# Attention beside a gated MLP: dense products on the whole TensorE array instead of four column tiles, and the second norm's scale spread by TensorE

## The chip, the cores and the metric

The kernel runs on one core of a Trainium2 chip. The time is device time in microseconds from the start to the end of the program on that core. Before the change it is 1151.72 us, the median of two runs (1150.81 and 1152.64). The core's engines run side by side, each with its own instruction stream in a fixed order: TensorE (PE, matrix products; its weight loads are listed apart as PEld), VectorE (DVE), ScalarE (ACT), GpSimd (POOL) and SyncE (SP), which here issues all DMAs. They wait for each other through semaphores.

## The reference, cut to what matters

There are 2048 tokens of 1024 features, in bf16. The input is normed once, and the result goes through an attention with 32 heads of 32 features and, normed a second time, through an MLP with 3584 hidden features. The MLP's output gates that of the attention.

```python
xn = layernorm(x)                                   # 2048 x 1024
q, k, v = split(xn @ wqkv)                          # 32 heads, 32 features each
p = softmax(q @ k.T * 32 ** -0.5)                   # per head, 2048 x 2048
s = (p @ v, heads side by side) @ wo
y = layernorm(xn)
h = gelu(y @ w1 + b1)                               # 2048 x 3584
g = silu(h @ w2 + b2)
out = x + s * g
```

The mean of xn is zero and its variance is known from the first norm, so the second norm is one factor per token. The kernel computes it from the first norm's statistics.

## The kernel before, in words

**Layout.** Activations are kept transposed, features on the partitions and tokens along the row: `xnT` (in the buffer `big`), `yT` (the second norm of 256 tokens), `hT` (hidden features). The 32 heads are handled in 8 groups of 4, since four heads of 32 features fill 128 partitions.

**Dense products.** All products with weight matrices (Q, K and V projections, `w1`, `w2`, `wo`) go through the helper `quad` (line 578). It cuts the 128 output partitions of one product into four column tiles of 32 and issues four matmuls at `tile_position=(0, 32 * j)`, each with 128 contracted rows, 32 weight columns and the same 256 or 512 moving columns. Each matmul has a weight load of its own. `quad` is also used where four heads really differ: for P times V (line 930) and for the column sums of P (`ones`, lines 939 and 942). The trace shows all of these as L580, told apart by the names of their tiles. The scores (line 912) run in row tiles, 32 rows by 128 columns for each of the four heads. The transposes of the start (line 691) use the whole array.

**Attention.** `unit` (line 901) is one step: four heads, 256 queries, 256 keys. It has eight score matmuls, two exponentials of 1024 elements per partition on ScalarE (line 921), one addition on VectorE that halves the work of the column sums (line 924), eight PV matmuls and four sum matmuls. There are 512 units. For each head group and block of 256 queries (64 in all) the PV and sum matmuls of eight units follow as one burst into one bank of PSUM; then `norm` (line 949) divides.

**MLP.** For each chunk of 256 tokens `make_y` (line 763) multiplies `xnT` by the second norm's factor into `yT`, `w1_item` (line 771) makes 256 hidden features at a time, with bias and GELU on VectorE and ScalarE, and `w2_item` (line 802) sums over all hidden features into 256 outputs, with the gate. The weights are read again for each chunk, through rings of three (`w1r`) and four (`w2r`) buffers.

**The second norm's factor and the biases.** GpSimd computes the factor for all tokens at the end of the start (lines 728 to 732), one token per partition and one column per block of 128 tokens. `yT` needs it along the row, the same on all partitions. So line 733 stores it to DRAM, token after token (`s_scratch`), and `make_y` reads 256 of them back, spread over all partitions, into the one buffer `sbc` (line 764). Line 734 reads the bias `b1` element by element into a layout with features on partitions (`b1T`), and line 735 reads `b2` to all partitions. These DMAs are issued on SyncE's queue in the order of the plan.

**What sets the order.** The program is not written in the order of its execution. Every instruction is registered with an estimate of its duration, its reads and its writes, and `_Plan.run` (line 78) places all of them by a list schedule on the host, each engine's stream in the order in which its instructions were placed. On TensorE a score step comes before a PV or sum step, and that before a dense step (a "chunk", mostly two quads). Score steps are held back while the dense work is behind its even share of all units. Each step on TensorE has a mode, "c" for column tiles, "r" for row tiles, "t" for the transposes; where it differs from the last one's, the planner adds 100 ns (line 278). Dense work and PV bursts both have the mode "c". From the end of the start on, PV bursts and dense items share two banks of PSUM, six are kept for scores. The semaphore waits follow from the order (`settle`, line 336), so the order is fixed before the kernel runs, whatever the durations on the chip.

## Time and profile before

| | |
|---|---|
| median of the runs | 1151.72 us (1150.81 to 1152.64) |
| the profiled execution's own time | 1151.67 us |
| its span, first to last instruction of the program | 1140.5 us |
| mean granted TensorE clock over the span | 0.991 |
| TensorE | 29,984 matmuls and as many weight loads |
| VectorE, ScalarE | 1543 and 1186 instructions |
| DMA | 159.55 MB, 140 GB/s over the span |

How to read the lines shown below. A group's line gives the source line, engine, operation, the tiles written and read with their shapes (partitions x elements, for matmuls rows*columns of the tile of the array used), how many there are, the busy time in us, the mean duration of one in ns, and the idle time of the engine just before them with what ended it. A line of the timeline gives start and length in us, engine, line, operation and count, and in brackets the idle time before it and its cause. A line of the waits gives who waited for whom, the total in us, how often, and the longest. A line of the windows gives a stretch, its length, each engine's busy time with its instructions (TensorE, weight loads, VectorE, ScalarE, GpSimd), the mean granted TensorE clock, and DMA. "issue" is time in which an engine waited for nothing that the profile shows. The line numbers are those of the kernel before. Matmuls overlap, so a matmul's duration is longer than the distance to the next.

### The profile page before, as it was taken

To read this page: it belongs to the slowest core of one execution; us is meant where nothing else is said; L and a number is where in the kernel's file an instruction comes from. 1 tells how busy PE (TensorE), PEld (TensorE's weight loads), DVE (VectorE), ACT (ScalarE), POOL (GpSimd) and SP (SyncE) were. 2 spreads that over 40 slices of the span, in tenths; PEclk is the share of its full clock that TensorE was granted. 3 is DMA by queue.
4 is the path that set the end of the run, shared out by engine and by line. 5 is a ranking of instruction groups with operands and counts; after the bars stand their busy time and mean duration, and the time that the engine had idled before them with its cause. 6 is when DMAs were issued, how large, how long until landed. Compare 5 with 4: busy or idle time off the path is not lost.

```text
span 1140.5 us, 63544 instructions
## 1 busy us (share of the span) xinstructions
PE 1046.8 (92%) x29984; PEld 714.6 (63%) x29984; DVE 853.4 (75%) x1543; ACT 1039.5 (91%) x1186; POOL 32.7 (3%) x42
## 2 busy tenths in 40 slices
PE   5769999999989999999999899999999998789997
PEld 4545666667766667667666567657766666566443
DVE  6559877687778867886669776976679777756786
ACT  3759989999989999999999999999999999879993
POOL 5600000000000000000000000000000000000000
PEclk9979999999999999999999999999999999899999
DMA  8243376434564556443555546533365458464442
GB/s 250 67 107 109 94 199 169 115 95 117 145 169 135 144 142 191 120 113 95 148 163 141 142 136 172 160 92 109 83 179 158 121 154 256 150 189 122 132 131 85
DMA packets 289268, 159.55 MB, mean 140 GB/s; under 512 B 28912, under 2 KB 278768, under 8 KB 289008
## 3 DMA queue, kind: packets, MB, share of 16 engines
q1 hardware_dynamic: 289008, 155.49, 47.8%
q8 instruction: 235, 3.85, 1.5%
q14 instruction: 25, 0.20, 0.1%
HBM read 143.40 MB, written 12.07 MB: 136 GB/s over the span
## 4 chain that ended last, share of the span: by engine, by line
PE 63%; ACT 27%; DVE 4%; issue 3%; SPq 1%; POOL 1%; DMA 1%; POOLq 0%; ACTq 0%
PE ps L580 53%; ACT P L921 25%; PE ps L912 10%; ACT ut L795 2%; DVE stats L704 1%; SPq L735 1%; DVE xb L787 1%; DVE nt L951 1%; POOL gw L718 0%; ACT gw L828 0%; DMA sbc<-s_scratch 0%; DVE V L653 0%; POOLq L1057 0%; DMA hT<-in_A_x_dram 0%; SPq L734 0%
## 5 line engine op out<-in xcount | busy, mean ns | idle before, releaser
L921 ACT ACTIVATE P<-ps 128x1024 bf16<-128x1024 f32 x1024 | 970.4, 1087 | 69.4 <-PE ps L912 47.0
L924 DVE TENSOR_TENSOR PA<-P 128x1024 bf16<-128x1024 bf16 x512 | 348.6, 688 | 117.5 <-ACT P L921 92.9
L580 PE MATMUL ps<-yT,w1r 128*32 128x256 bf16 x7168 | 235.9, 274 | 10.2 <-issue 6.7
L580 PE MATMUL ps<-w2r,hT 128*32 128x256 bf16 x7168 | 230.3, 273 | 8.6 <-issue 5.4
L580 PEld LDWEIGHTS ps<-yT,w1r 128*32 128x32 bf16 x7168 | 179.5, 97 | 52.9 <-issue 35.5
L580 PEld LDWEIGHTS ps<-w2r,hT 128*32 128x32 bf16 x7168 | 181.2, 97 | 41.7 <-issue 32.4
L580 PE MATMUL ps<-P,V 128*32 128x256 bf16 x4096 | 161.6, 276 | 12.1 <-DVE V L653 8.6
L580 PE MATMUL ps<-big,qk 128*32 128x512 bf16 (+1 forms) x2208 | 133.7, 369 | 5.4 <-DVE xb L787 3.1
L580 PE MATMUL ps<-qk,big 128*32 128x256 bf16 (+1 forms) x2944 | 126.4, 307 | 6.2 <-ACT big L694 2.0
L580 PEld LDWEIGHTS ps<-P,V 128*32 128x32 bf16 x4096 | 109.5, 98 | 28.0 <-DVE V L653 9.3
L912 PE MATMUL ps<-qk 32*128 32x256 bf16 x2048 | 105.0, 275 | 21.8 <-ACT P L921 14.8
L580 PE MATMUL ps<-PA,ones 128*32 128x256 bf16 x2048 | 120.7, 275 | 3.2 <-issue 3.0
L912 PE MATMUL ps<-QKT 32*128 32x256 bf16 x2048 | 102.7, 273 | 11.5 <-ACT P L921 9.8
L580 PEld LDWEIGHTS ps<-qk,big 128*32 128x32 bf16 x2944 | 72.6, 97 | 40.9 <-issue 14.3
L787 DVE TENSOR_TENSOR xb<-ps,b1T 128x512 bf16<-128x512 f32 x112 | 76.8, 686 | 18.7 <-PE ps L580 17.7
L580 PEld LDWEIGHTS ps<-big,qk 128*32 128x32 bf16 x2208 | 53.8, 97 | 53.4 <-issue 13.7
L912 PEld LDWEIGHTS ps<-qk 32*128 32x128 bf16 x2048 | 31.3, 92 | 87.8 <-ACT P L921 58.6
L797 DVE SCALAR_TENSOR_TENSOR hT<-ut,xb 128x512 bf16<-128x512 f32 x112 | 76.4, 684 | 9.5 <-ACT ut L795 9.3
L912 PEld LDWEIGHTS ps<-QKT 32*128 32x128 bf16 x2048 | 30.7, 92 | 81.1 <-ACT P L921 67.2
L795 ACT ACTIVATE ut<-ut 128x512 f32<-128x512 f32 x112 | 77.8, 698 | 2.8 <-DVE ut L793 2.8
L793 DVE SCALAR_TENSOR_TENSOR ut<-sq,xb 128x512 f32<-128x512 bf16 x112 | 76.7, 686 | 1.7
L580 PEld LDWEIGHTS ps<-PA,ones 128*32 128x32 bf16 x2048 | 55.6, 97 | 19.3 <-issue 16.9
(50 smaller groups left out, 443.8 us busy)
## 6 DMA issues: line engine op xcount, KB each, us to landing
w1r<-in_B_w_dram SPq DMA_DIRECT2D x112, 512.0 KB, 4.3
w2r<-in_B_w_dram SPq DMA_DIRECT2D x128, 448.0 KB, 4.5
qk<-in_A_wqkv_dram SPq DMA_DIRECT2D x16, 256.0 KB, 3.6
g_scratch<-gw SPq DMA_DIRECT2D x32, 128.0 KB, 2.7
o_scratch<-ot SPq DMA_DIRECT2D x56, 64.0 KB, 3.1
big<-o_scratch SPq DMA_DIRECT2D x7, 512.0 KB, 7.3
hT<-in_A_x_dram SPq DMA_DIRECT2D x10, 256.0 KB, 5.4
qk<-in_A_wqkv_dram SPq DMA_DIRECT2D x4, 512.0 KB, 4.5
```

Of the source, the lines that this page charges most:

```text
L580: ins = e.matmul(dst(j), lhsT=lhsT(j), rhs=rhs(j), start=start, stop=stop, tile_position=(0, 32 * j), skip_group_check=True)
L704: dve(lambda e, t=t, c=c: e.bn_stats(stats[:, t, c, :], xst[t][:, c * 512:(c + 1) * 512]), 600, [XS(t)], [("st", t, c)], 1)
L735: dma("b2", lambda e: e.dma_start(b2b[:], B_b2.rearrange("(o d) -> o d", o=1).to_broadcast([128, D])), 262144, [("s3",)], [("b2",)])
L787: dve(lambda e: e.tensor_tensor(xb_t[i3][:].rearrange("p (k t) -> p k t", k=2), bank(it.bank).rearrange("p (k t) -> p k t", k=2), b1T[:, 2 ...
L793: dve(lambda e: e.scalar_tensor_tensor(ut_t[i3][:], sq_t[p % 2][:], 1.0 / GA, xb_t[i3][:], op0=ALU.add, op1=ALU.mult), c_f32(512), [("sq", ...
L795: act(lambda e: e.activation(ut_t[i3][:], ut_t[i3][:], ACT.Tanh, scale=GC * GA), c_act(512), [("ut", i3)], [("ut", i3)], 1)
L797: dve(lambda e: e.scalar_tensor_tensor(hT[:, hs].rearrange("p k t -> p (k t)"), ut_t[i3][:], 1.0, xb_t[i3][:], op0=ALU.add, op1=ALU.mult), ...
L912: ins = e.matmul(bank(b0[j], kk * 256, (kk + 1) * 256), lhsT=QKT[sl][32 * j:32 * j + 32, 1, kb * 128:(kb + 1) * 128], rhs=QKT[sl][32 * j:3 ...
L921: x = act(lambda e, h=h: e.activation(P[pi][:, 2 * h:2 * h + 2].rearrange("p j k q -> p (j k q)"), ps[:, pr[h] * 1024:(pr[h] + 1) * 1024], ...
L924: pa = dve(lambda e: e.tensor_tensor(PA[ai][:], P[pi][:, :, 0, :], P[pi][:, :, 1, :], op=ALU.add), c_b16(1024), [("P", pi, 0), ("P", pi, 1 ...
L951: a = dve(lambda e: e.transpose(nt_t[i][:], bank(pv.bank, 256, 512)), c_ps(256), [], [("nt", i)], 1, pv)
```

## The change

1. Every dense product (V, Q and K projections, `w1`, `w2`, `wo`) is one matmul on the whole array, 128 weight columns, through a new helper `full`, in place of four on column tiles. PV and the sums keep `quad`. The dense chunks' mode becomes "f", that of the transposes too. PV and sums keep "c".
2. The second norm's factor no longer goes through DRAM. For each block of 128 tokens VectorE multiplies an f32 identity by the factor (a diagonal, `dg`), TensorE multiplies it by a matrix of ones in f32 (two matmuls of 128 columns into one bank), and VectorE copies the result to `sbc`. This is an item of the MLP's queue, once for each of the eight chunks.
3. `b1` is read as 28 rows of 128 into `b1r`, which needs only the identity to be ready in the plan, is transposed on TensorE, and copied to `b1T`.

```diff
-        s_d = nc.dram_tensor("s_scratch", (S,), F32).ap()
...
+        b1r = sb("b1r", [FB, 128], BF16)
+        identf = sb("identf", [128, 128], F32)
+        onesf = sb("onesf", [128, 128], F32)
+        dg = sb("dg", [128, 2, 128], F32)
...
-        def chunk(item, fn, occ, R, mode="c", W=()):
+        def chunk(item, fn, occ, R, mode="f", W=()):
...
+        def full(e, dst, lhsT, rhs, start, stop):
+            return e.matmul(dst, lhsT=lhsT, rhs=rhs, start=start, stop=stop, skip_group_check=True)
...
+        dve(lambda e: e.tensor_single_scalar(identf[:], iota_i[:], 0, op=ALU.is_equal), 220, [("iota",)], [("identf",)], 2)
+        dve(lambda e: e.memset(onesf[:], 1.0), 140, [], [("onesf",)], 2)
...
-                        ins = quad(e, lambda j: bankp(b, j, t2 * 256, (t2 + 1) * 256),
-                                   lambda j: xnT[:, dc, tb * 128 + 32 * j:tb * 128 + 32 * j + 32],
-                                   lambda j: wv[:, dc, :], dc == 0, dc == DC - 1)
+                        ins = full(e, bank(b, t2 * 256, (t2 + 1) * 256), xnT[:, dc, tb * 128:(tb + 1) * 128],
+                                   wv[:, dc, :], dc == 0, dc == DC - 1)
...
-            chunk(it, fn, 620, [("xnb", t % 4), ("ident",)], mode="t")
+            chunk(it, fn, 620, [("xnb", t % 4), ("ident",)])
...
-        dma("s_st", lambda e: e.dma_start(s_d.rearrange("(t p) -> p t", p=128), lnp[:, :, 3]), 8192, [("s3",)], [("s_d",)])
-        dma("b1", lambda e: e.dma_start(b1T[:], B_b1.rearrange("(fb p) -> p fb", p=128)), 8192, [("s3",)], [("b1",)])
+        dma("b1", lambda e: e.dma_start(b1r[:], B_b1.rearrange("(fb p) -> fb p", p=128)), 8192, [("ident",)], [("b1r",)])
...
+        def b1_item():
+            it = _Item("mlp")
+            chunk(it, lambda e, b: e.transpose(bankb(b)[:, 0:FB], b1r[:], ident[0:FB, 0:FB]), 60, [("b1r",), ("ident",)])
+            dve(lambda e: e.tensor_copy(b1T[:], bankb(it.bank)[:, 0:FB]), c_ps(FB), [], [("b1",)], 0, it)
+            mq.append(it)
+
         def make_y(c):
-            dma("sbc", lambda e: e.dma_start(sbc[:], s_d[c * 256:(c + 1) * 256].rearrange("(o d) -> o d", o=1).to_broadcast([128, 256])),
-                131072, [("s_d",)], [("sbc",)])
+            for i in range(2):
+                dve(lambda e, i=i: e.tensor_scalar_mul(dg[:, i, :], identf[:], lnp[:, 2 * c + i, 3:4]), 140,
+                    [("s3",), ("identf",)], [("dg", i)], 2)
+            it = _Item("mlp")
+
+            def fn(e, b):
+                for i in range(2):
+                    ins = full(e, bank(b, i * 128, (i + 1) * 128), onesf[:], dg[:, i, :], True, True)
+                return ins
+            chunk(it, fn, 500, [("dg", 0), ("dg", 1), ("onesf",)])
+            dve(lambda e: e.tensor_copy(sbc[:], bank(it.bank, 0, 256)), c_ps(256), [], [("sbc",)], 0, it)
+            mq.append(it)
...
         for s_ in seq_mlp():
             if s_[0] == "y":
+                if s_[1] == 0:
+                    b1_item()
                 make_y(s_[1])
```

The other dense products (the pairs of Q and K in the start, `w1`, `w2`, `qk_item`, `wo`) change from `quad` to `full` as the V product above does.

More of the change, by code (lines that the diff above doesn't have):

```diff
@@ L781, in fn @@
                     for dc in dcs:
[L782 to L784 removed]
+                        ins = full(e, bank(b, f2 * 256, (f2 + 1) * 256), w1r[gi][:, dc, f2 * 128:(f2 + 1) * 128],
+                                   yT[:, dc, :], dc == 0, dc == DC - 1)
                     return ins
```

22 lines of the change are left out of this document (7 added, 15 removed).

## The prediction

> **What bounds the kernel now.** I read the page first (span, busy shares, the chain that ended last), then the waits by engine, then the timeline around the longest waits.
>
> ```profile
> span 1140.5 us, 63544 instructions
> PE 1046.8 (92%) x29984; PEld 714.6 (63%) x29984; DVE 853.4 (75%) x1543; ACT 1039.5 (91%) x1186; POOL 32.7 (3%) x42
> q8 instruction: 235, 3.85, 1.5%
> PE 63%; ACT 27%; DVE 4%; issue 3%; SPq 1%; POOL 1%; DMA 1%; POOLq 0%; ACTq 0%
> ```
>
> TensorE and ScalarE are both over 90% busy, and the chain runs mostly over TensorE. So a microsecond of TensorE counts, until ScalarE has no gap left. How much ScalarE gives is in the waits. The first two rows are its waits from 140 to 1040 us, the others TensorE's and one of VectorE's in the whole span:
>
> ```profile
> ACT P L921 <- PE ps L912: 32.7, 46, 4.7
> ACT P L921 <- PE ps L580: 7.5, 12, 1.9
> ...
> PE ps L912 <- ACT P L921: 24.6, 34, 1.9
> PE ps L580 <- issue: 17.3, 29, 1.4
> ...
> PE ps L912 <- issue: 7.3, 9, 3.3
> DVE yT L767 <- DMA sbc<-s_scratch: 13.5, 1, 13.5
> ```
>
> In the long middle ScalarE waits 32.7 + 7.5 = 40.2 us for TensorE. That is the most that a lighter TensorE can win there. TensorE itself loses 17.3 + 7.3 = 24.6 us to "issue", where no semaphore held it. One of those stops is the 3.3 us in the start, the other 21.3 us lie in the middle and end.
>
> What those stops are is seen where two follow each other (timeline of TensorE):
>
> ```profile
> 956.46 0.28 PE L580 MATMUL ps<-PA,ones 128*32 128x256 bf16 x1 [1.26 <-issue]
> 956.47 0.50 PE L580 MATMUL ps<-P,V 128*32 128x256 bf16 x8
> 956.69 0.71 PE L580 MATMUL ps<-PA,ones 128*32 128x256 bf16 x16
> 957.33 0.40 PE L912 MATMUL ps<-qk 32*128 32x256 bf16 x8
> 957.66 1.71 PE L580 MATMUL ps<-w2r,hT 128*32 128x256 bf16 x56
> 959.30 0.40 PE L912 MATMUL ps<-qk 32*128 32x256 bf16 x8
> 959.63 0.51 PE L580 MATMUL ps<-w2r,hT 128*32 128x256 bf16 x12
> 959.97 0.71 PE L580 MATMUL ps<-yT,w1r 128*32 128x256 bf16 x18
> 962.07 0.61 PE L580 MATMUL ps<-yT,w1r 128*32 128x256 bf16 x14 [1.39 <-issue]
> ```
>
> Both stops fall inside a group of four (18 is not a multiple of 4), where the program has no wait. Between them lie 1 + 8 + 16 + 8 + 56 + 8 + 12 + 18 = 127 matmuls, each with a weight load: 254 instructions. The page's instruction queue moved 3.85 MB in 235 packets, 16.4 KB each; over the 59,968 instructions of TensorE that is 64 bytes apiece and 255 a packet. So TensorE stops at the end of a packet of its own code, when the next is late.
>
> **The start** has one long hole:
>
> ```profile
> 44.42 2.95 POOL L732 TENSOR_TENSOR lnp<-lnp,mhalf 128x16 f32<-128x16 f32 x1
> 50.24 9.36 SPq L735 DMA_DIRECT2D b2b<-in_B_b_dram  x1
> ...
> 56.66 0.58 PE L912 MATMUL ps<-qk 32*128 32x256 bf16 x5 [3.33 <-issue]
> 59.64 0.43 SPq L764 DMA_DIRECT2D sbc<-s_scratch  x1
> 63.44 1.90 DVE L767 TENSOR_TENSOR yT<-big,sbc 128x512 bf16<-128x512 bf16 x3 [13.48 <-DMA sbc<-s_scratch]
> 65.99 1.90 PE L580 MATMUL ps<-P,V 128*32 128x256 bf16 x32 [7.78 <-DVE V L653]
> ```
> ```profile
> s_scratch<-lnp SPq DMA_DIRECT2D x1, 8.0 KB, 11.3
> b1T<-in_B_b_dram SPq DMA_DIRECT2D x1, 7.0 KB, 13.9
> ```
> ```profile
> 60.00:80.00 20.00, 13.21 (x340) 8.81 (x344) 11.40 (x21) 8.43 (x9) 0.00 (x0) 0.75 0.34 95
> ```
>
> The scale is ready at 44.42 + 2.95 = 47.37. It then goes to DRAM as single words (8 KB take 11.3 us), beside a bias read element by element (7 KB, 13.9 us). SyncE is stuck 9.36 us in the next issue, the scale comes back at 63.4, and VectorE stands 13.48 us in front of yT with the V cast behind it. TensorE stands 3.33 + 7.78 = 11.1 us, and the granted clock falls to a mean of 0.75 from 60 to 80 us (row above).
>
> **The change part by part.**
>
> *Scale and biases.* The store, the eight broadcasts and the word-wise bias read go, so SyncE is free for the b2 and weight loads behind them. In their place VectorE waits for the same POOL result, makes two diagonals, TensorE multiplies, VectorE copies, yT follows. Queued behind the new wait on VectorE are the K and V casts and the PA additions, and TensorE waits for those. VectorE was free for yT at 63.44 - 13.48 = 49.96, later than 47.37, so I expect under 1 us of wait. TensorE gets back its 11.1 us. The slow clock also goes: it weighs only on the 13.2 us that TensorE worked between 60 and 80, 0.25 x 13.2 = 3.3 us; I take 3. Together **-14 us**. Bounds: -3 (only the 3.33 us stop, if VectorE waits elsewhere) and -19 (the 13.48 us of VectorE in full, and 0.25 x 20 = 5 us of clock). The bias read, now 28 whole rows, goes out behind the input loads; the turn is one small matmul and one copy, which hide in the start: nothing (0.5 us if not).
>
> *The seven later scales.* Their broadcasts were hidden (the waits name sbc once, in the start), so what replaces them is a pure cost. No row shows an f32 matmul. A pair of 128 columns costs at least two bf16 ones of the same size, 2 x 0.057 = 0.11 us (the cadence below), and I bound it above by two of four times the columns, 2 x 4 x 0.057 = 0.46 us. The bank is then held by a copy like
>
> ```profile
> L682 DVE CAST qk<-ps 128x256 bf16<-128x256 f32 x8 | 3.3, 416 | 2.9 <-PE ps L580 2.9
> ```
>
> so 0.11 to 0.46 + 0.42 = 0.88 us each, 0.9 to 7 us for eight. I take **+4**, the middle, since attention work fills part of the bank's wait. (The Trainium skill, "FP8 and Floating Point Precision", counts true FP32 as four passes; by it the pair is 0.46 us.) VectorE's 8 x about 0.9 us lies in its 25% of idle time.
>
> *Dense products, instruction for instruction.*
>
> ```profile
> 1017.66 6.29 PE L580 MATMUL ps<-w2r,hT 128*32 128x256 bf16 x224
> 500.19 1.71 PE L580 MATMUL ps<-yT,w1r 128*32 128x256 bf16 x56
> 501.83 0.40 PE L912 MATMUL ps<-QKT 32*128 32x256 bf16 x8
> 43.18 1.06 PE L580 MATMUL ps<-big,qk 128*32 128x256 bf16 x32
> 44.17 0.62 PE L691 MATMUL ps<-ident,gw 128*128 128x128 bf16 x8
> 34.96 0.62 PE L691 MATMUL ps<-ident,gw 128*128 128x128 bf16 x8
> 35.51 0.73 PE L580 MATMUL ps<-big,qk 128*32 128x256 bf16 x20
> ```
>
> 56 groups of four take 6.29 us, with 0.27 for the last one's own length: 6.02 / 55 = 0.109 us a group. Each group's four tiles run together. The transposes are the only full-array work: eight take 0.62 us with 0.22 for the last: 0.40 / 7 = 0.057 us for 128 columns with a 128x128 weight load inside. 256 columns at the same rate are 0.11 us. So the arithmetic gains **0**, and the larger weight load is hidden.
>
> *Switches.* Groups to full array: 43.18 to 44.17 is 0.99 for eight groups (0.87), so 0.11 more. Full array to groups: 34.96 to 35.51 is 0.55 for eight (0.45), 0.10 more. Groups to scores: 500.19 to 501.83 is 1.64 for 14 groups (1.53), 0.11. Score blocks keep their price. But dense and PV products, which now share one tiling, will differ, and each place where they meet costs 0.10. Through the whole timeline I count 119 such places, the first at 65.99 (above), the last:
>
> ```profile
> 1125.14 0.82 PE L580 MATMUL ps<-qk,big 128*32 128x512 bf16 x12
> 1125.78 0.28 PE L580 MATMUL ps<-PA,ones 128*32 128x256 bf16 x4
> 1125.89 1.04 PE L580 MATMUL ps<-qk,big 128*32 128x512 bf16 x16
> ```
>
> 119 x 0.101 = **+12 us**, bounds +6 and +24 (the planner is run anew and may halve or double the meetings). Against it, the stagger inside a group (0.11 to a switch against 0.10 from the full array, some 0.011) goes before each score block that follows dense work; 500.19 and 501.83 show one, and I count 414 of the 512 blocks: **-4.6**, bounds 0 and -5.
>
> *Code.* Dense matmuls are 29,984 - 512 x 20 (scores, PV, sums) - 128 = 19,616; a quarter stays, so 14,712 matmuls and as many loads go and about half of TensorE's 59,968 instructions remain. A packet of 127 matmuls lasted 127 / 4 x 0.109 = 3.5 us in dense groups; it will last 13.9. Only packets filled with PV groups still run as fast as now. I take **-20** of the 21.3 us, bounds 0 and -24 (the chain between 140 and 1040 us has 2.7% of issue, below).
>
> ```profile
> by line: PE ps L580 52.2%; ACT P L921 29.9%; PE ps L912 10.6%; issue 2.7%; ACT ut L795 1.9%; DVE xb L787 0.7%; DVE nt L951 0.6%; ACT gw L828 0.5%; DVE nr L952 0.2%; DVE hT L797 0.2%; DVE nb L954 0.2%; DVE qk L880 0.1%; DVE PA L924 0.1%; DVE
> ```
>
> 0.027 x 900 = 24 us lies on the path itself, which is why I let the gain through to the end. The Trainium skill, "Runtime: NRT & Kernel Launch", section "Instruction fetch mechanics", says the crossing of such a 16 KiB boundary is mostly hidden. By that rule this term is nothing and the sum 1149; the trace here, with 127 matmuls between stops of 1.26 and 1.39 us, disagrees.
>
> **Sum**, against the profiled execution's 1151.67 (span 1140.5 and 11.2 around it, within 0.1 of the median 1151.72): -14 + 4 + 0 + 12 - 4.6 - 20 = -22.6, **1129 us**, 2.0% faster.
>
> **The rivals.**
>
> *The code stops stay, or ScalarE takes the gain* (1149 us, chance 0.18): without the -20. For it: TensorE already waits 24.6 us for ScalarE, so it sometimes runs ahead. Against it: ScalarE's 40.2 us of waiting.
>
> *The hole only moves* (1140, chance 0.14): the new chain does not do what it says, because the diagonals stand on VectorE earlier than yT did, ahead of casts that TensorE needs, and wait for the same POOL step. Then only the 3.33 us stop goes: 1151.7 - 3 + 4 + 12 - 4.6 - 20. For it: POOL ends only at 47.37, and VectorE is strictly in order. Against: the 49.96 above.
>
> *More than forecast* (1115, chance 0.13): the start gives 19, the code 24, the scales cost 1, the meetings 6 to 12.
>
> *Slower* (1181, chance 0.05): the sums of P wait for VectorE's additions, and the planner puts dense matmuls between them, as at 1125.78. Each such pair costs two switches. Eight more meetings in each of the 64 bursts (8 head groups x 8 query blocks) are 512 x 0.101 = 52 us. It makes the kernel slower than before from 22.6 / 0.101 = 224 more meetings on, 3.5 a burst. Against it: the burst at 956.47 to 957.33 runs unbroken, and the present 119 are under two a burst.
>
> **How the numbers follow.** The forecast has the remaining 0.50. 2% is 23 us, to 1128.7, and is about what a measurement of this kernel can tell from no change. The forecast lies at that border: half of it, with the larger gain, makes faster 0.38; slower 0.04 (most of its rival); within 2% 0.58. The range reaches from below the larger gain's time to just past the rival without the code gain: 1110 to 1152.
>
> **What would show it.** TensorE near 15,300 matmuls and about 120 packets in the instruction queue; the two "issue" rows under 5 us together; no wait on sbc from DRAM, the first w1 product near 60 us instead of 75.07, the clock at 1.00 from 60 to 80; TensorE's meetings near 119 at 0.10 each. It is wrong if the issue rows fall and ScalarE's waits for TensorE do not, or if VectorE shows a new wait of several microseconds for the POOL step.

## The result and the profile after

The changed kernel takes **1119.15 us**, the median of two runs (1117.59 and 1120.72), against 1151.72 before: 32.6 us less, a ratio of 0.9717 with a 95% interval of 0.965 to 0.9784. The forecast was 1129, in a range of 1110 to 1152. So direction and range held, and the time is 10 us below the forecast. The steps below show that this closeness is partly luck: one term was far too small, and a loss that the sum did not have took most of the difference back.

The rows of the changed kernel's page that answer to those of before:

```profile
span 1115.4 us, 34138 instructions
PE 1038.8 (93%) x15238; PEld 669.1 (60%) x15305; DVE 860.3 (77%) x1570; ACT 1034.9 (93%) x1186; POOL 32.5 (3%) x42
q8 instruction: 120, 1.97, 0.7%
ACT 57%; PE 37%; DVE 4%; POOL 1%; issue 1%; POOLq 0%; DMA 0%
```

Line numbers shift from kernel to kernel. The scores are L912 before and L932 in the changed kernel, the exponentials L921 and L941, `quad` L580 and L583, the new helper `full` L588; the tiles named beside them tell them apart in every kernel.

TensorE has half its instructions (15,238 matmuls for 29,984), the code comes in 120 packets for 235, and the chain that ended last now runs mostly over ScalarE, which held 27% of it before and holds 57% now. TensorE's share fell from 63% to 37%, and issue's from 3% to 1%.

The waits over the whole span, changed kernel:

```profile
ACT P L941 <- PE ps L932: 44.9, 28, 5.3
...
PE ps L932 <- ACT P L941: 34.1, 43, 1.9
...
DVE dg L776 <- POOL lnp L738: 4.6, 1, 4.6
PE ps L588 <- issue: 4.5, 27, 0.3
```

The issue row still says 4.5 us, but none of its 27 places is longer than 0.3 us: 15,305 weight loads stand beside 15,238 matmuls, and the 27 places are where records of matmuls are missing. The fourth kernel below, whose trace lost none, has no issue row for TensorE. So the stops at the ends of packets no longer show here at all.

Since ScalarE is now the engine with the least to spare, the span is best read as its busy time and its idle time. The view by windows, for ScalarE alone (stretch, its length, ScalarE's busy time with its instructions, mean granted TensorE clock, DMA share, GB/s), first before, then changed:

```profile
0.00:100.00 100.00, 62.03 (x69) 0.93 0.53 142
100.00:900.00 800.00, 769.66 (x885) 1.00 0.49 136
900.00:1000.00 100.00, 93.14 (x107) 0.97 0.59 179
1000.00:1140.50 140.50, 114.69 (x128) 1.00 0.43 133
```
```profile
0.00:100.00 100.00, 75.59 (x85) 1.00 0.54 157
100.00:900.00 800.00, 782.55 (x905) 1.00 0.48 136
900.00:1000.00 100.00, 84.78 (x99) 0.90 0.61 183
1000.00:1115.40 115.40, 91.92 (x101) 0.99 0.39 121
```

Length less busy time is the idle time of each stage. It went from 38.0 to 24.4 us in the start, from 30.3 to 17.4 in the long middle, from 6.9 **up** to 15.2 between 900 and 1000, and from 25.8 to 23.5 in the end: 20.5 us less in all. ScalarE's own busy time fell by 4.6 (1039.5 to 1034.9). Together that is the 25.1 us between the spans 1140.5 and 1115.4. The medians are 32.6 apart because the execution of before whose trace is shown was a quick one: the timed run of 1151.67 has a core span of 1149.9, and other executions of that kernel reach from 1145.5 to 1165.1. With the 2 us that the others have around their spans the shown one would stand near 1142.5, below every timed one. So the row of before in the table below sums to about 9 us less than that of the timed execution would.

### The profile page after: what moved, and what is told of

It is laid out like the page before. It is cut to its first block, busy times and chain, and to the rows that moved or that the text cites. A ratio compares the mean times of both kernels' runs of the same rounds, so it can differ in the third digit from the quotient of the medians.

```text
span 1115.4 us, 34138 instructions
## 1 busy us (share of the span) xinstructions
PE 1038.8 (93%) x15238; PEld 669.1 (60%) x15305; DVE 860.3 (77%) x1570; ACT 1034.9 (93%) x1186; POOL 32.5 (3%) x42
## 4 chain that ended last, share of the span: by engine, by line
ACT 57%; PE 37%; DVE 4%; POOL 1%; issue 1%; POOLq 0%; DMA 0%
ACT P L941 52%; PE ps L588 24%; PE ps L583 7%; PE ps L932 6%; ACT ut L815 3%; ACT gw L847 1%; POOL gw L724 1%; DVE PA L944 1%; DVE stats L710 0%; DVE nt L971 0%; DVE xb L807 0%; POOLq L1075 0%; ACT big L700 0%; DMA hT<-in_A_x_dram 0%; DVE hT L817 0%
## 5 line engine op out<-in xcount | busy, mean ns | idle before, releaser
L941 ACT ACTIVATE P<-ps 128x1024 bf16<-128x1024 f32 x1024 | 977.3, 1142 | 47.4 <-PE ps L932 44.9
L588 PE MATMUL ps<-yT,w1r 128*128 128x256 bf16 x1792 | 232.3, 275 | 3.6 <-DVE xb L807 2.1
L588 PE MATMUL ps<-w2r,hT 128*128 128x256 bf16 x1792 | 224.6, 274 | 3.6 <-DVE hT L817 1.8
L588 PEld LDWEIGHTS ps<-yT,w1r 128*128 128x128 bf16 x1792 | 163.3, 98 | 60.3 <-issue 29.7
L588 PEld LDWEIGHTS ps<-w2r,hT 128*128 128x128 bf16 x1792 | 164.5, 98 | 52.1 <-issue 26.4
L583 PE MATMUL ps<-P,V 128*32 128x256 bf16 x4096 | 159.4, 276 | 0.8 <-DVE yT L1056 0.6
L588 PE MATMUL ps<-qk,big 128*128 128x256 bf16 (+1 forms) x718 | 120.3, 306 | 8.3 <-issue 1.9
L588 PE MATMUL ps<-big,qk 128*128 128x512 bf16 (+1 forms) x504 | 119.7, 367 | 8.5 <-issue 2.4
L932 PE MATMUL ps<-qk 32*128 32x256 bf16 x2048 | 102.3, 274 | 20.9 <-ACT P L941 19.8
L583 PE MATMUL ps<-PA,ones 128*32 128x256 bf16 x2048 | 118.0, 276 | 0.0
L932 PE MATMUL ps<-QKT 32*128 32x256 bf16 x2048 | 102.6, 275 | 16.1 <-ACT P L941 14.3
L583 PEld LDWEIGHTS ps<-P,V 128*32 128x32 bf16 x4096 | 102.0, 97 | 25.6 <-issue 9.5
L588 PEld LDWEIGHTS ps<-qk,big 128*128 128x128 bf16 x736 | 65.6, 98 | 48.4 <-issue 15.9
L815 ACT ACTIVATE ut<-ut 128x512 f32<-128x512 f32 x112 | 86.3, 773 | 2.9 <-DVE ut L813 2.9
L807 DVE TENSOR_TENSOR xb<-ps,b1T 128x512 bf16<-128x512 f32 x112 | 76.8, 685 | 15.6 <-PE ps L588 14.6
L588 PEld LDWEIGHTS ps<-big,qk 128*128 128x128 bf16 x552 | 48.4, 99 | 57.1 <-issue 14.7
L932 PEld LDWEIGHTS ps<-qk 32*128 32x128 bf16 x2048 | 30.4, 92 | 84.4 <-ACT P L941 77.9
L932 PEld LDWEIGHTS ps<-QKT 32*128 32x128 bf16 x2048 | 30.4, 92 | 82.4 <-ACT P L941 75.3
L583 PEld LDWEIGHTS ps<-PA,ones 128*32 128x32 bf16 x2048 | 53.1, 97 | 14.9 <-issue 13.3
```

What stands on the lines that cost most here:

```text
L583: ins = e.matmul(dst(j), lhsT=lhsT(j), rhs=rhs(j), start=start, stop=stop, tile_position=(0, 32 * j), skip_group_check=True)
L588: return e.matmul(dst, lhsT=lhsT, rhs=rhs, start=start, stop=stop, skip_group_check=True)
L807: dve(lambda e: e.tensor_tensor(xb_t[i3][:].rearrange("p (k t) -> p k t", k=2), bank(it.bank).rearrange("p (k t) -> p k t", k=2), b1T[:, 2 ...
L815: act(lambda e: e.activation(ut_t[i3][:], ut_t[i3][:], ACT.Tanh, scale=GC * GA), c_act(512), [("ut", i3)], [("ut", i3)], 1)
L932: ins = e.matmul(bank(b0[j], kk * 256, (kk + 1) * 256), lhsT=QKT[sl][32 * j:32 * j + 32, 1, kb * 128:(kb + 1) * 128], rhs=QKT[sl][32 * j:3 ...
L941: x = act(lambda e, h=h: e.activation(P[pi][:, 2 * h:2 * h + 2].rearrange("p j k q -> p (j k q)"), ps[:, pr[h] * 1024:(pr[h] + 1) * 1024], ...
```

## The experiments

Three theories had to be told apart. **Code**: the gain comes from the stops at the ends of TensorE's code packets, which whole-array products make half as many and far apart. **Start**: it comes from the hole around 50 to 66 us, which the new way of the scale closes. **Order**: it comes from the plan, which was made anew and puts all instructions in another order. Since any change of an estimate gives a new order, the sharpest experiments keep the order of one kernel and exchange only what is executed.

All runs, with ScalarE's idle time by stage, worked out as above from each kernel's windows (us). e1 to e4, e5 to e8, e9 to e11, and e12 ran on one chip each, and share the runs of before there, whose medians were 1149.14, 1154.96, 1153.82 and 1155.11. Between these groups the ratios compare better than the medians.

| run | median | ratio to before (95%) | 0-100 | 100-900 | 900-1000 | rest |
|---|---|---|---|---|---|---|
| before | 1151.72 | | 38.0 | 30.3 | 6.9 | 25.8 |
| changed | 1119.15 | 0.9717 (0.965-0.9784) | 24.4 | 17.4 | 15.2 | 23.5 |
| e1_dense_only | 1120.44 | 0.9734 (0.9694-0.9773) | 36.7 | 16.2 | 8.1 | 23.4 |
| e2_scale_only | 1148.79 | 0.998 (0.9951-1.001) | 27.7 | 34.3 | 9.8 | 33.8 |
| e3_new_order_column_tiles | 1161.11 | 1.0094 (1.0061-1.0126) | 27.5 | 43.4 | 9.2 | 34.3 |
| e4_old_order_whole_array | 1118.01 | 0.9722 (0.9694-0.9751) | 40.6 | 11.0 | 9.6 | 21.0 |
| e5_old_order_whole_array_row_loads | 1105.26 | 0.9565 (0.9531-0.9598) | 26.0 | 11.8 | 11.6 | 19.7 |
| e6_old_order_column_tiles_row_loads | 1148.48 | 0.993 (0.9898-0.9961) | 29.8 | 41.5 | 7.2 | 30.3 |
| e7_small_weight_loads | 1117.66 | 0.967 (0.963-0.971) | 39.5 | 11.2 | 11.6 | 23.3 |
| e8_changed_planned_as_one_mode | 1112.59 | 0.9629 (0.9595-0.9662) | 27.3 | 12.6 | 12.2 | 22.8 |
| e9_whole_array_scale_in_runs | 1107.58 | 0.9584 (0.9557-0.961) | 29.0 | 10.4 | 10.1 | 19.6 |
| e10_changed_scale_cost_640 | 1116.63 | 0.9667 (0.9637-0.9697) | 24.6 | 16.4 | 14.5 | 23.5 |
| e11_changed_slack_20 | 1125.34 | 0.9741 (0.9706-0.9776) | 23.4 | 17.0 | 15.9 | 34.1 |
| e12_changed_bf16_scale_product | 1118.24 | 0.9679 (0.9651-0.9707) | 24.8 | 17.4 | 15.3 | 23.5 |

### The two parts, each alone

The first kernel is the changed one with scale and bias taken back to the DMAs of before:

```diff
-            chunk(it, fn, 500, [("dg", 0), ("dg", 1), ("onesf",)])
-            dve(lambda e: e.tensor_copy(sbc[:], bank(it.bank, 0, 256)), c_ps(256), [], [("sbc",)], 0, it)
...
+            dma("sbc", lambda e: e.dma_start(sbc[:], s_d[c * 256:(c + 1) * 256].rearrange("(o d) -> o d", o=1).to_broadcast([128, 256])),
+                131072, [("s_d",)], [("sbc",)])
```

> Only the dense products change (whole array); the scale still goes through DRAM and the bias is still read by elements. Theory (code): the gain of the dense part is that TensorE no longer stops for its own code: about -22 us, against +12 us for the meetings of dense and PV work and -4.6 us for the stagger, so about 15 us under the kernel before; TensorE's issue waits in the middle fall from 20.5 us to under 5; the wait for sbc (13.5 us) stays. Rival (order): the planner's new order is the gain, and then this kernel keeps it too, but so does the new order with column tiles (third run). Rival (start): nearly all of the change is the start, and this one is within 5 us of the kernel before.

Measured: 1120.44 us, as fast as the whole change within what is measured, and 28.7 us under before on its chip, about twice the expected 15. The hole of the start is still there (36.7 us idle in the first 100). The waits of VectorE and of TensorE:

```profile
DVE yT L768 <- DMA sbc<-s_scratch: 12.8, 1, 12.8
```
```profile
PE ps L580 <- issue: 2.8, 2, 1.4
```

The two stops that are left stand at 57.0 and 58.7 us, inside the start's hole; in the middle there is none.

The second is the changed kernel with `full` taken back to `quad` in every dense product (and mode "c" for them), so that it holds only the new scale and bias rows:

```diff
-                        ins = full(e, bank(b, f2 * 256, (f2 + 1) * 256), w1r[gi][:, dc, f2 * 128:(f2 + 1) * 128],
-                                   yT[:, dc, :], dc == 0, dc == DC - 1)
+                        ins = quad(e, lambda j: bankp(b, j, f2 * 256, (f2 + 1) * 256),
+                                   lambda j: w1r[gi][:, dc, f2 * 128 + 32 * j:f2 * 128 + 32 * j + 32],
+                                   lambda j: yT[:, dc, :], dc == 0, dc == DC - 1)
```

> Only the scale by TensorE and the bias rows change; dense products stay four matmuls on column tiles. Theory: the start gives 13 to 15 us (the 32nd exponential falls from 84.2 us to about 70), the eight pairs cost 1 to 5 us later, and TensorE's issue waits stay near 20 us in the middle: 9 to 14 us under the kernel before. Rival (start alone): 25 us or more under it. Rival (the start's gain is eaten later, since ScalarE or the planner's pace takes it): within 4 us of it.

Measured: 1148.79, a ratio of 0.998 whose interval holds 1, so the expected 9 to 14 us did not come, and the rival that the gain is eaten later held. The stops are still there (30.7 us of issue). The start is 10.3 us better (27.7 for 38.0 us of idle), and the middle, the stretch to 1000 and the end are 4.0, 2.9 and 8.0 worse; some 9 us of these 14.9 are the quick execution in before's trace. Start alone does not explain the gain.

### The order, crossed with the array

The third kernel has the changed kernel's order to the last instruction, and only issues four column-tile matmuls where that issues one:

```diff
+        def four(e, dst, lhsT, rhs, start, stop):
+            for j in range(4):
+                ins = e.matmul(dst[32 * j:32 * j + 32], lhsT=lhsT[:, 32 * j:32 * j + 32], rhs=rhs, start=start, stop=stop,
+                               tile_position=(0, 32 * j), skip_group_check=True)
+            return ins
...
-                        ins = full(e, bank(b, f2 * 256, (f2 + 1) * 256), w1r[gi][:, dc, f2 * 128:(f2 + 1) * 128],
+                        ins = four(e, bank(b, f2 * 256, (f2 + 1) * 256), w1r[gi][:, dc, f2 * 128:(f2 + 1) * 128],
```

> The changed kernel's plan, to the instruction, but each dense product is issued as four matmuls on column tiles again, so only the instructions differ. Theory (code): the packets of code are late again, issue waits of 20 us or more come back; the switches between dense and PV work (112 of them) no longer cost 0.10 us each. Together 10 to 15 us slower than the changed kernel, about 1132. Rival (order): the order is what gained, issue waits stay small, and without the 11 us of switches it is faster than the changed kernel, about 1110.

The fourth is the opposite: before's order and modes, with `full` in place of `quad` in all dense products:

```diff
-                        ins = quad(e, lambda j: bankp(b, j, f2 * 256, (f2 + 1) * 256),
-                                   lambda j: w1r[gi][:, dc, f2 * 128 + 32 * j:f2 * 128 + 32 * j + 32],
-                                   lambda j: yT[:, dc, :], dc == 0, dc == DC - 1)
+                        ins = full(e, bank(b, f2 * 256, (f2 + 1) * 256), w1r[gi][:, dc, f2 * 128:(f2 + 1) * 128],
+                                   yT[:, dc, :], dc == 0, dc == DC - 1)
```

> The kernel before, plan and order unchanged (the planner is told that dense and PV work share a mode, which is no longer so), scale and bias as before, but each dense product is one matmul on the whole array. Theory (code): like the first run, 10 to 18 us under the kernel before, with issue waits under 5 us in the middle and 119 meetings at 0.10 us. Rival (order): the order is the gain and is missing here, so 7 us slower than the kernel before (12 for the meetings, less 4.6).

Measured: 1161.11 for the new order with column tiles, 42 us above the changed kernel (10 to 15 were expected) and 0.6 to 1.3% above before; 1118.01 for the old order with the whole array, 31 us under before on its chip (10 to 18 were expected). So the **order theory falls**: the new order alone gains nothing, and the whole array alone is the gain. Waits of TensorE and ScalarE in the third kernel, then in the fourth:

```profile
PE ps L592 <- issue: 18.6, 26, 2.8
PE ps L583 <- issue: 10.2, 12, 1.7
...
PE ps L938 <- issue: 3.0, 4, 1.2
...
ACT P L947 <- PE ps L938: 71.6, 67, 5.1
```
```profile
PE ps L910 <- ACT P L919: 22.2, 30, 1.9
PE ps L580 <- DVE V L655: 14.7, 2, 13.9
...
ACT P L919 <- PE ps L910: 29.1, 20, 6.8
```

With column tiles the stops add up to 18.6 + 10.2 + 3.0 = 31.8 us on three lines, and ScalarE starves behind them (71.6 us). With the whole array in before's order there is no issue row left for TensorE, while the start's hole still stands (13.9 us of waiting for the V cast).

Since the fourth kernel differs from before in nothing but the matmuls, TensorE's stream can be compared place by place. Adding up, over all steps, the distance between two starts beyond the cadence and the switch, where nothing released the second, gives 48.7 us before and 12.8 in the fourth kernel. Some 8 to 9 us of both are stretches at half the granted clock, so the difference of 36 us is the part that the matmuls explain. It stands against the 24.6 of the issue rows: the rows count only the end of each stop that no earlier matmul covers, and leave out the short ones.

### Is it the code, and why is it late?

If the stops are late code packets, they need something that delays them. The weights are read again for every 256 tokens and fill the DMA queues. The next kernel is before, with its column tiles, order and 235 packets, but the later weight loads bring only one part in eight of `w1` and one in seven of `w2`:

```diff
-            dma(f"w1{gi}", lambda e: e.dma_start(w1r[gi][:], src), 524288, [], [("w1", gi)])
+            dma(f"w1{gi}", lambda e: e.dma_start(w1r[gi][:], src) if p < NW1R else e.dma_start(w1r[gi][:, 0:1], src[:, 0:1]), 524288, [], [("w1", gi)])
...
-            dma(f"w2{i}", lambda e: e.dma_start(w2r[:, i], src), 458752, [], [("w2", i)])
+            dma(f"w2{i}", lambda e: e.dma_start(w2r[:, i], src) if n_ < NW2R else e.dma_start(w2r[:, i, 0:1], src[:, 0:1]), 458752, [], [("w2", i)])
```

> The kernel before in the same order, but after the first three w1 and four w2 loads each later one brings only the first 128-row slice (an eighth and a seventh of the bytes); the rest of each buffer is stale, so the MLP is left wrong. Theory (code packets are late because they queue behind the weights' traffic): TensorE's issue waits fall from 24.6 us to under 10, and the time by 15 to 30 us. Rival (a packet takes longer to fetch than the densest 127 matmuls take to run, whatever the traffic): issue waits stay at 18 us or more and the time within 6 us of the kernel before.

Measured: 1117.66, with column tiles, as fast as the whole array in the same order (1118.01). Windows of the long middle, before and in this kernel (after the clock: DMA share and GB/s), and this kernel's page and waits:

```profile
140.00:1010.00 870.00, 816.89 (x24216) 573.18 (x24211) 665.25 (x1181) 832.17 (x957) 0.00 (x0) 1.00 0.51 145
```
```profile
140.00:1010.00 870.00, 833.22 (x24776) 588.35 (x24778) 678.04 (x1202) 843.48 (x976) 0.00 (x0) 0.98 0.15 43
```
```profile
q8 instruction: 235, 3.85, 1.5%
```
```profile
PE ps L580 <- issue: 4.3, 4, 1.8
```

DMA traffic fell from 145 to 43 GB/s, the code is the same 235 packets, and the stops fell from 38 to 5 (4 here, one of 1.1 us at a score step), from 24.6 us to 5.4. In neither trace does TensorE wait for a weight load, so the smaller loads do not win by landing sooner. So neither the matmuls nor their number is the cost by itself: what costs is that a packet of 127 matmuls is worked off in about 3.5 us while its successor shares the DMA with the weights. Either fewer instructions or less traffic cures it.

That the stops are late packets can be read off the traces' records of single DMA packets. In before, 37 of the 38 stops end 1.2 to 1.6 us after the end of an instruction packet, though such packets come about 4.5 us apart; in e2, e3 and e6 all of the 45, 42 and 42 stops end 1.2 to 1.7 us after one. Of the 27 places of the changed kernel's issue row only 3 lie so. The exceptions, the stop of 3.3 us in before and two in e7 (1.1 and 1.3 us), all stand in the start's hole, as do the two of e1; what those are is open. A packet's own transfer takes as long with the traffic as without, in the median 1.07 us in before and 1.12 in e7. So the delay comes before the transfer, and what holds it there is not shown.

### Why does the start's gain not arrive?

The changed kernel is no faster than dense products alone, although its first 100 us are 12 us better. To see a better start without a new order, the scale's store and the bias read of the fourth kernel, and of before, get the shape of rows, 64 and 56 bytes to a partition (factors and biases then stand at the wrong tokens and features):

```diff
-        dma("s_st", lambda e: e.dma_start(s_d.rearrange("(t p) -> p t", p=128), lnp[:, :, 3]), 8192, [("s3",)], [("s_d",)])
-        dma("b1", lambda e: e.dma_start(b1T[:], B_b1.rearrange("(fb p) -> p fb", p=128)), 8192, [("s3",)], [("b1",)])
+        dma("s_st", lambda e: e.dma_start(s_d.rearrange("(p t) -> p t", p=128), s3t[:]), 8192, [("s3",)], [("s_d",)])
+        dma("b1", lambda e: e.dma_start(b1T[:], B_b1.rearrange("(p fb) -> p fb", p=128)), 8192, [("s3",)], [("b1",)])
```

> As the fourth run (old order, whole array, scale through DRAM), but the scale is stored and the bias read in runs of 64 and 56 bytes instead of single words; the order of every engine is the same to the instruction. The scale's tokens and the bias then stand in the wrong places, so those two are left wrong. Theory (the start's gain is real, and the new plan loses it again): in the same order an earlier start carries through, so 12 to 17 us under the fourth run, about 1104. Rival (absorbed): ScalarE is the bound after the start, catches up in any case, and the time stays within 4 us of the fourth run, about 1118.

> The kernel before with that edit alone (same order, column tiles; scale and bias in the wrong places). Theory: the hole at 50 to 66 us closes, 11 to 15 us under the kernel before, about 1136. Rival (absorbed): within 4 us of the kernel before, as the second run was.

With the whole array (e5): 1105.26 against 1118.01, by the ratios 1.6% less. The spans of the traces say the same, 1104.0 against 1117.0, and in the stages the start gives 14.6 us of ScalarE's idle time and the rest takes only 1.5 back. **In an unchanged order the start's gain arrives.** The store and the bias read change together in e5 and e6, so which of the two made the hole is not shown. With column tiles (e6): 1148.48 against 1154.96 on the same chip, ratio 0.993. That is 6.5 us by the medians, short of the 11 to 15 expected and more than the 4 of the rival. In its trace the start's 8.2 us are outweighed by 11.2 more in the middle, where the stops have grown from 24.6 to

```profile
PE ps L581 <- issue: 25.1, 36, 2.3
...
PE ps L913 <- issue: 5.4, 6, 1.6
```

30.5 us; but some 9 us of the comparison are the quick execution in before's trace.

So the new order of the changed kernel must lose what its start wins. Three kernels keep its instructions and change a number of the plan only (in e8 the plan also swaps one of VectorE's 512 additions for four more sum matmuls): dense products and PV planned as one mode (mode "c" for the dense ones, "t" for transposes), a planned cost of 640 ns in place of 500 for the scale item, and a slack of 20 units in place of 10 by which dense work may lag:

```diff
-        def chunk(item, fn, occ, R, mode="f", W=()):
+        def chunk(item, fn, occ, R, mode="c", W=()):
```
```diff
-            chunk(it, fn, 500, [("dg", 0), ("dg", 1), ("onesf",)])
+            chunk(it, fn, 640, [("dg", 0), ("dg", 1), ("onesf",)])
```
```diff
-        plan.run(HG * 64, 10)
+        plan.run(HG * 64, 20)
```

> The changed kernel, but the planner is told, as in the kernel before, that dense and PV work share a mode, so it adds nothing for their meetings and comes to another order; the instructions are the same. Theory (the later loss is a matter of the plan): the start stays as in the changed kernel (32nd exponential near 70 us) and the time differs from 1119 by 4 us or more, either way. Rival (absorbed): within 3 us of it.

> The changed kernel with one number of the plan changed: the planned cost of each of the eight scale products is 640 ns in place of 500, nearer to what they take. No instruction is added or removed, only the order can shift. Theory (what the changed kernel loses after its start is luck of the list schedule): the time moves by 3 us or more, most likely down, since 1119 is the worst of the three plans seen with the whole array and a short start. Rival (the scale products themselves cost the 13 us): it stays within 3 us of 1119.

> The changed kernel, with the score steps allowed to run 20 units ahead of the dense work's even share in the plan, in place of 10. Theory (ScalarE is now near its bound, and loses time where scores are held back for dense work, 15.2 us of gaps between 900 and 1000 us): those gaps move or shrink and the time falls by 3 to 10 us. Rival (the plan's pace is not what bounds): within 3 us of 1119, or slower because dense work is left for the end.

Measured: 1112.59, 1116.63 and 1125.34. e8 moved as its theory said. e10 moved by 2.5 us, inside the 3 us of its rival. e11 became 6 us slower where 3 to 10 faster was expected, as its rival allows. The last two ran on one chip, and their intervals do not meet. So all but the same instructions take times up to 13 us apart (0.9629 to 0.9741 of before) by numbers that exist only on the host. One more suspect is the scale's f32 products themselves. They are taken out by a kernel in the changed order that multiplies two bf16 matrices there (the factor is then wrong):

```diff
-                    ins = full(e, bank(b, i * 128, (i + 1) * 128), onesf[:], dg[:, i, :], True, True)
+                    ins = full(e, bank(b, i * 128, (i + 1) * 128), ident[:], ident[:], True, True)
```

> The changed kernel with the same order of every engine, but each of the sixteen f32 products of the scale is replaced by one bf16 product of the same size (identity by identity), so the second norm's factor is left wrong. It prices the f32 arithmetic by itself. The trace of the changed kernel shows 0.53 us for a pair from its start to the next work, against 0.11 for two bf16 ones. Theory (what the changed kernel loses after its start lies in the plan's order): 1 to 4 us under it, 1115 to 1118, with the gaps of ScalarE between 900 and 1000 us as they are. Rival (the f32 products cost the 13 us): 8 us or more under it, 1111 or less.

Measured: 1118.24, within the scatter of the changed kernel's 1117.59 to 1120.72, with the same idle times in every stage to 0.4 us. So the loss is not in these products, and it changes with the order.

Where the order loses it is seen in one row of the waits. TensorE's wait for ScalarE in front of a score step, where the bank to write is not yet read, in the kernel of the old order with the good start (e5), then in e8, e10 and e11:

```profile
PE ps L911 <- ACT P L920: 22.5, 31, 1.9
```
```profile
PE ps L932 <- ACT P L941: 27.3, 37, 1.9
```
```profile
PE ps L932 <- ACT P L941: 30.4, 38, 1.9
```
```profile
PE ps L932 <- ACT P L941: 38.8, 47, 1.9
```

With 34.1 for the changed kernel, the order of these waits is the order of the times: 22.5, 27.3, 30.4, 34.1, 38.8 us beside 1105.3, 1112.6, 1116.6, 1119.2, 1125.3. (Two do not fit their places to a microsecond or two: e12, 35.5 us and 1118.2, and the last kernel below, 21.2 us and 1107.6. e1 and e4, with 22.9 and 22.2 us, have the hole in the start and cannot be compared.) From e5 to the changed kernel they grow by 11.6, and the span by 11.4. I read it so: a score step that stands too early in the fixed order holds back the dense work behind it, and TensorE, idle for only 76.6 us of the span, is late for later scores. That is argued from this agreement; no run shows it by itself.

The table narrows down what in the plan does it. Between 100 and 900 us ScalarE is idle for 16.2 to 17.4 us in all whole-array kernels that are planned with a price between dense and PV work (changed, e1, e10, e11, e12), and for 10.4 to 12.6 in those planned as one mode (e4, e5, e8, e9). Between the changed kernel and e8, which differ in this price, dense and PV products meet 112 and 120 times in the traces: the price saves eight meetings of 0.10 us and goes with 4.8 us more idle time in this stage. Why a true price leads to a worse order is not shown.

Between 900 and 1000 us the clock has a part too. The granted clock there is 0.90 in the changed kernel, 0.97 before and 0.93 in e5. Timeline of the changed kernel:

```profile
943.79 0.40 PE L932 MATMUL ps<-qk 32*128 32x256 bf16 x8 [1.94 <-ACT P L941]
946.14 0.40 PE L932 MATMUL ps<-qk 32*128 32x256 bf16 x8 [1.94 <-ACT P L941]
...
947.97 0.61 PE L932 MATMUL ps<-qk 32*128 32x256 bf16 x8 [1.11 <-ACT P L941]
948.51 3.17 PE L588 MATMUL ps<-yT,w1r 128*128 128x256 bf16 x14
```

After three score steps that wait for ScalarE with almost no dense work between them, 14 dense products take 3.17 us, about 0.21 us each where they take 0.109 at the full clock. This can bear on the 3.6 us of idle time that the changed kernel has above e5 in this stage, not on the 5.6 us between 100 and 900, where the granted clock is 1.00 in both. No run separates the clock from the order.

In e11 the slack adds a plain second loss: at the 512th exponential's start it has done about 130 of some 2,830 dense products (of 256 columns) fewer than the changed kernel, and what is left over makes the stage after 1000 us idle for 34.1 us.

### The best of both

The last kernel puts together what had won: dense products on the whole array planned as one mode, `b1` in rows and turned on TensorE, and the scale through DRAM again, but in runs of 128 bytes after one 32x32 transpose on VectorE:

```diff
+        pool(lambda e: e.tensor_tensor(s3t[:, 0:NT], lnp[:, :, 2], mhalf[:, :], op=ALU.pow), 2700, [("s2",), ("mhalf",)], [("s3",)], 2)
+        dve(lambda e: e.transpose(s3r[:], s3t[:]), 110, [("s3",), ("s3z",)], [("s3r",)], 1)
+        s_v = s_d.rearrange("(t b q) -> b t q", b=4, q=32)
+        for b in range(4):
+            dma(f"s_st{b}", lambda e, b=b: e.dma_start(s_v[b], s3r[32 * b:32 * b + NT, :]), 2048, [("s3r",)], [("s_d", b)])
```

> A version meant to beat both: dense products on the whole array, planned as one mode with PV; the scale still goes through DRAM, but VectorE turns it first in 32x32 blocks, so that it is stored in runs of 128 bytes; the bias by rows and TensorE, as in the changed kernel. No f32 matmuls, and one new operation on VectorE. Theory (the start's gain carries through when the middle is not planned worse): 1102 to 1112 us, at or below the eighth run's 1113. Rival (the plan is luck, and a few new operations turn it): anywhere from 1105 to 1122.

Measured: **1107.58**, ratio 0.9584 (0.9557 to 0.961), below the changed kernel's interval. Waits of VectorE and TensorE:

```profile
DVE yT L781 <- DMA sbc<-s_scratch: 4.1, 1, 4.1
```
```profile
PE ps L925 <- ACT P L934: 21.2, 29, 1.9
```

The scale costs 4.1 us of VectorE's time in the start, about what the diagonals wait for GpSimd in the changed kernel, and the order is as good as before's. So the scale need not go over TensorE; it is enough that neither it nor the bias travels in single words.

## Why the prediction came out as it did

**Code, -20: the mechanism right, the size wrong.** This is the term that was mis-sized. The working took the issue rows' 21.3 us as the whole cost and bounded it at -24. In the same order the stream shows 48.7 us going to 12.8, -36, because the rows leave out what is covered and what is short. And the trace shown was a quick execution of before: in medians the fourth kernel gains 31 us although it pays the same 12 us of switches and gains nothing in the start, which makes the code worth an estimated 31.1 + 12 - 4.6 = 38.5 us there. The rival "the code stops stay, or ScalarE takes the gain" is refuted for the first half; ScalarE did become the longest part of the chain, but only after the gain. The Trainium skill, "Runtime: NRT & Kernel Launch", section "Instruction fetch mechanics", which calls these crossings mostly hidden, agrees with the kernel whose weight traffic is cut (5.4 us of issue in the waits) and disagrees with before, where the fetch shares the DMA with 145 GB/s.

**Start, -14: right in the start, wrong at the end.** This is the step that failed: the gain was carried through to the end as if the order stayed. ScalarE's idle time in the first 100 us fell by 13.6, and the 32nd exponential starts at 69.4 us for 84.2. But against the fourth kernel, which has neither the new start nor a new order, the changed kernel's 16.2 us less of idle in the start is met by 6.4, 5.6 and 2.5 us more in the later stages: 14.5 taken back. The prediction had noted that the planner is run anew, but used it only for the count of the switches.

**"Under 1 us of wait" on VectorE: wrong.** The diagonals were placed earlier than `yT` had been. Timeline of the changed kernel's start:

```profile
44.34 2.94 POOL L738 TENSOR_TENSOR lnp<-lnp,mhalf 128x16 f32<-128x16 f32 x1
...
47.31 0.48 DVE L776 TENSOR_SCALAR dg<-identf,lnp 128x128 f32<-128x128 f32 x2 [4.63 <-POOL lnp L738]
...
48.45 0.39 PE L588 MATMUL ps<-qk,big 128*128 128x256 bf16 x2 [1.41 <-DVE V L660]
...
49.23 1.94 ACT L941 ACTIVATE P<-ps 128x1024 bf16<-128x1024 f32 x2 [2.72 <-PE ps L932]
...
59.79 0.71 PE L588 MATMUL ps<-dg,onesf 128*128 128x128 f32 x4
60.43 0.40 PE L932 MATMUL ps<-qk 32*128 32x256 bf16 x8
...
63.28 0.61 PE L588 MATMUL ps<-yT,w1r 128*128 128x256 bf16 x4
```

VectorE stands 4.63 us for GpSimd, as the rival "the hole only moves" said and as the prediction had named among its signs of being wrong, and the V cast behind it costs TensorE 1.41 and ScalarE 2.72 us. It is a much smaller hole than the 7.78 it replaces, and nothing else of the chain is slow: the first `w1` product comes at 63.28 (75.07 before), and the clock from 60 to 80 us is 1.00:

```profile
60.00:80.00 20.00, 18.98 (x272) 12.89 (x273) 19.70 (x41) 17.93 (x22) 0.00 (x0) 1.00 0.48 137
```

**Scales, +4: the pieces about right, their cost not seen.** The copy takes 411 ns as assumed. The f32 pair takes 60.43 - 59.79 = 0.64 us, less 0.11 for the switch, 0.53: just above the upper bound of 0.46. Replacing it by bf16 changes the time by less than the runs scatter; no run takes out the copies and diagonals by themselves in one order, so the +4 as a whole is not shown.

```profile
L776 DVE TENSOR_SCALAR dg<-identf,lnp 128x128 f32<-128x128 f32 x16 | 4.2, 279 | 4.6 <-POOL lnp L738 4.6
L785 DVE COPY sbc<-ps 128x256 f32<-128x256 f32 x8 | 3.3, 411 | 0.0
```

**Cadence, 0, switches, +12, and stagger, -4.6: right.** The longest dense run of the changed kernel is the twin of the one shown of before, 56 products in 6.28 us for 56 groups in 6.29:

```profile
984.68 6.28 PE L588 MATMUL ps<-w2r,hT 128*128 128x256 bf16 x56
```

Dense and PV products meet 60 + 52 = 112 times, for 119 before. A meeting takes 0.202 to 0.205 us from start to start, against 0.099 to 0.109 inside one tiling: 0.10 each, 11 us. From the start of the last dense step to a score block it is 0.205 us in the median, for 0.216 before, the 0.011 of the stagger. The rival "slower", with more meetings, did not come near. The rival "more than forecast", at 1115, names the nearest time, but by a gain of 19 in the start, which the order took back, and of 24 in the code, which was 36.

**The 11.2 us around the span** were a misreading: the trace and the time 1151.67 belong to two executions. In all later runs the time is about 2 us above the core's span. So the sum should have been set against the spans: -22.6 forecast, -25.1 measured. That the two agree hides -36 for -20 in the code against 14.5 us lost to the order.

## What to carry to other kernels

When an engine stops with no semaphore to wait for, count its instructions between two stops: if it is a full packet of code each time, the same arithmetic in fewer, larger instructions can win even if not one cycle of the array is saved; here column tiles with little weight traffic on the DMA were as fast; the stops that a waits view lists are a lower bound of what they cost. A gain in the start of a program whose order is planned on the host is worth nothing until the order is the same: compare the two in one order, and look at what each plan makes the busiest engines wait for, and at the granted clock behind those waits. A small transfer in single words can hold up the large ones beside it, and turning it on an engine first, so that it moves in runs of 128 bytes, was enough here, with the bias read by rows as well.

## What the runs showed of the hardware that was not expected

- The scatter of the executions goes with the code stops. With column tiles and full weight traffic, times on one chip spread over 9.8 us for before (19 runs, 1145.5 to 1155.3) and 20 for the third kernel (10 runs, 1150.8 to 1170.5). With the whole array they stay within 2.1 (e4), 1.5 (e5), 5.6 (e1) and 5.7 (e9), with column tiles and little weight traffic within 3.8 (e7); these are only four to six runs each.
- ScalarE's own busy time, for the same 1186 instructions, is 1039.5 to 1041.5 us in the column-tile kernels with 38 or more stops and 1033.4 to 1035.3 in the others, e7 with its column tiles among the latter. What makes its instructions longer is not shown.
- In before, e2, e3 and e6, 166 of the 167 stops without a semaphore end 1.2 to 1.7 us after the end of an instruction packet, while the transfer of such a packet takes 1.04 to 1.12 us in the median in every column-tile kernel, with 145 GB/s of traffic or 43.
- An f32 product of 128 columns is recorded as two matmuls, and the pair takes 0.53 us, nearly five times the 0.11 us that 256 columns take in bf16.
- The word-wise transfers delayed others too: reading `b2` to all partitions took 12.8 us to land before and 3.4 to 3.9 us in the changed kernel, e2, e5, e6 and e9, which have none; the store of the 8 KB of factors took 11.3 us in words, and in runs of 64 bytes 1.9 (e5) and 3.5 (e6).
